# ELU applied to the loaded values of the last layer instead of the evicted ones of the first

## The chip, the cores and the metric

The kernel runs on one core of a Trainium2 chip. Times are device microseconds (us) of that core for one execution. TensorE (PE) does the matrix products, with its weight loads shown apart as PEld; VectorE (DVE), ScalarE (ACT) and GpSimd (POOL) work on elements; SyncE (SP) issues nearly all DMAs. Each engine takes its instructions in the order in which the program holds them.

## What is computed

Attention over 4 x 12 heads with RMS-normed queries and keys gives x (1792 tokens x 768). A capacity-limited mixture of 8 experts maps x to x again. The last stage is two dense layers with an ELU between them, on all tokens:

```python
def _moe2_ref(x, w_in, w_out):          # x 1792 x 768, w_in 768 x 2048, w_out 2048 x 768
    h = x @ w_in
    g = np.where(h > 0.0, h, 1.0 * (np.exp(np.minimum(h, 0.0)) - 1.0))
    return (g @ w_out).astype(np.float32)
```

The change touches this last stage, and a few instructions at the very start of the attention.

## The kernel before

The program runs in three stages: attention up to about 270 us, routing and experts up to about 540 us, the two dense layers to the end. Every float32 operand is split into a high and a low float16 part, and each product is three matmuls: high x high, high x low, low x high.

**Layer 1** (`winograd` called from `fewer`, and `plain`) computes h, transposed: its 2048 rows in pairs f = 0..7 of two 128-row blocks r, its 896 + 896 token columns in two halves h. The first 512 columns of each half go through seven products instead of eight (`winograd`): the accumulators a, b, c take the products in the order A11·B11 into b, A12·B21 into a, S2·T2 onto b, S3·T3 into c, S1·T1 onto b, A22·T4 onto c, S4·B22 onto b. Between them b is copied out twice (`snap`: p1 after the first product, u2 after S2·T2), c once (p7), and each of those copies must be done before the next product goes onto the same accumulator. `add` joins an accumulator with a copy on VectorE, `copy` takes the last one. The other 384 columns go through `plain`, four accumulators of 18 matmuls for each f, spread between the products.

Every finished piece of h (64 pieces: 32 of 512 columns, 32 of 384) goes through `elu`: ACT computes Exp into a tile e, ACT computes Relu(1 - e), DVE takes min(-h, that), which is minus ELU. Then SP stores e to a DRAM buffer `g_d`, laid out by groups of 128 token columns. The tiles e come from five buffers. Two homes for the copies lie in `kept`, inside the tile `sums` (the S operands of layer 1). While layer 1 runs, the weights of both layers are prepared on DVE and ACT.

**Layer 2** takes the tokens in seven groups g of 128 columns of each half. `operands(g)` loads four 128 x 1024 tiles q (one for each k = h + 2r) back from `g_d`, forms four sums s on DVE, and splits seven operands into high (ACT, L1133) and low (DVE, L1134) parts. `layer2` runs the same `winograd` with 24 matmuls of 384 columns for each product; `snap` there is L1245, `add` L1249, `copy` L1252. For g = 0 the piece f = 7 is not loaded but taken from the tiles e that still lie on the chip (`late`), so the sums and splits of g = 0 come in two parts, 7/8 and 1/8.

Three blocks of layer-2 weights come from the DRAM buffer `t_d` just before layer 2: T4 into the old place of x (`xc`), T3 and T1 into the tile `ex`, which takes the place of `sums`, each 1.5 MB. DMAs of SP start in program order, and a DMA whose source is still being stored waits, with all behind it.

The dense layers are placed on the engines by a scheduler: the order within an engine is not the order in the code. `issue_after` holds some instructions back behind another one. The attention's order, in contrast, is written out by hand. At its start a filler (`spin`, L97 to L102) runs 14 matmuls of 512 columns on zeros while the first inputs load.

Of the kernel before, what the change touches and what calls it, by code (L numbers as in the profile page):

```python
# [2 lines left out]

# [3 lines left out]
F32 = mybir.dt.float32  # L7
# [38 lines left out]
def attention(tc, qk_d, v_d, qT_d, idh, idn_d, R_d, xs, L, route, W, npairs=NP_):  # L46
    nc = tc.nc
    order, ramp = ([(s.split(":")[0], int(s.split(":")[1])) for s in x.split()] for x in (ORDER, RAMP))
    with tc.tile_pool(name="ac", bufs=1) as cp, \
# [35 lines left out]
        def first():  # L85

            d = ld[0]
            qk = d["qk"]
            d["r"] = sp.tile([P, 14], F32, tag="r", name="r0", bufs=6)
            sq = d["sq"] = sp.tile([P, 14, D], F32, tag="sq", name="sq0", bufs=1)  # L90
            khl = d["khl"] = sp.tile([P, 7, 2, D], F16, tag="khl", name="khl0")
            for n in ("ss", "ln", "y", "nt"):
                d[n] = sp.tile([P, 14], F32, tag=n, name=n + "0", bufs=4)
            warm, z = pp.tile([P, 512], F32, tag="o", name="warm", bufs=1), ql[1]
            nc.vector.memset(z[:, 0:512], 0.0)

            def spin(n):  # L97
                for _ in range(n):
                    nc.tensor.matmul(warm, z[:, 0:P], z[:, 0:512], start=True, stop=True)

            steps["w"] = spin
            spin(14)  # L102
            for x in (*xh_, *xl_):
                nc.gpsimd.memset(x[:, 448:512], 0.0)
            nc.gpsimd.tensor_tensor(G, idn_[:, P:P + 1], idn_[:, P + 1:P + 2], ALU.mult)
            nc.gpsimd.tensor_scalar(G, G, 0.125 * SQ, None, ALU.mult)
            nc.gpsimd.tensor_tensor(sq[:, Q], qk[:, Q], qk[:, Q], ALU.mult)
            nc.vector.tensor_tensor(sq[:, K], qk[:, K], qk[:, K], ALU.mult)
# [785 lines left out]
def moe(tc, xp, homes, xs, idx, idh, W, rows, ring, w1_d, w2_d, wi_d, wo_d, lin, g_d, t_d, out):  # L894
    nc = tc.nc
    with tc.tile_pool(name="mp", bufs=1, space=PSUM, reuse_waits="tile") as pp:
# [182 lines left out]
        with tc.tile_pool(name="wb", bufs=1, reuse_waits="tile") as wp:  # L1079
# [25 lines left out]
            def operands(g, late=None):  # L1105


                q = [ring.tile([P, 8, P], F32, tag="w2", name=f"q{g}_{k}", bufs=6) for k in (0, 2, 1, 3)]
                s = [W.wstage.tile([P, 8, P], F32, tag="wst", name=f"s{g}_{k}", bufs=5) for k in range(4)]

                n = 7 if late else 8
                for x, k in zip(q, (0, 2, 1, 3)):
                    nc.sync.dma_start(x[:, 0:n], g_d[g, k, :, 0:n])
                    if g == 1:
                        yield
                parts = [(slice(0, n), [x[:, 0:n] for x in q])]
                if late:
                    parts.append((slice(7, 8), [late[k][:, 0:P].unsqueeze(1) for k in (0, 2, 1, 3)]))
                todo, ahead = [], elus[-1].ins if late else None
                held = lambda n: tc.issue_after(ahead) if late and n else ExitStack()  # L1120
                for n, (f, (a11, a12, a21, a22)) in enumerate(parts):
                    s1, s2, s3, s4 = [x[:, f] for x in s]
                    with held(n):
                        nc.vector.tensor_tensor(s1, a21, a22, ALU.add)
                        nc.vector.tensor_tensor(s2, s1, a11, ALU.subtract)
                        nc.vector.tensor_tensor(s3, a11, a21, ALU.subtract)
                        nc.vector.tensor_tensor(s4, a12, s2, ALU.subtract)
                    todo.append((f, dict(zip((A11, A12, S2, S3, S1, A22, S4), (a11, a12, s2, s3, s1, a22, s4)))))
                a = {}

                def split(k, x):
                    for f, z in todo:
                        nc.scalar.activation(x[:, f, 0], z[k], AF.Copy, scale=SG)  # L1133
                        nc.vector.scalar_tensor_tensor(x[:, f, 1], z[k], SG, x[:, f, 0], ALU.mult, ALU.subtract)  # L1134
# [12 lines left out]

            elus = []

            with tc.tile_pool(name="l1", bufs=1, side="right", reuse_waits="tile") as sp:  # L1150
                def elu(f, cb, k, ps, done=False):
# [7 lines left out]
                    return e, nc.sync.dma_start(g_d[g, k, :, f].rearrange("g p c -> p g c"), e.rearrange("p (g c) -> p g c", c=P))  # L1159

                def plain(f):
                    n = CB[1][1] - CB[1][0]
                    for h, r in ((0, 0), (0, 1), (1, 0), (1, 1)):
                        t, bufs = PS[2 - r]
                        ps = pp.tile([P, 512], F32, name=f"l{f}_1{h}{r}", tag=t, bufs=bufs)[:, 0:n]
                        w = wic[f + 8 * r]
                        for d in range(6):
                            for m, (i, j) in enumerate(((0, 0), (0, 1), (1, 0))):
                                nc.tensor.matmul(ps, w[:, i, d * P:(d + 1) * P], xc[1][:, h, d, j], start=d == 0 and m == 0, stop=d == 5 and m == 2)  # L1169
                        yield elu(f, 1, 2 * r + h, ps)[1]  # L1170

                def fewer(f, beside):
                    made = {}
                    x = {A11: xc[0][:, 0, 0:3], A12: xc[0][:, 0, 3:6], A22: xc[0][:, 1, 3:6]} | dict(zip((S1, S3, S2, S4), (sums[0][:, k] for k in range(4))))
                    w = {B11: (f, 0), B21: (f, 384), B22: (f + 8, 384), T1: ((f, 1), 0), T2: ((f, 1), 384), T3: ((f, 3), 0), T4: ((f, 3), 384)}

# [6 lines left out]
                        if p in (A11, S2, S3, A22):  # L1183
                            next(beside)

                    homes = [*kept, sp.tile([P, 512], F32, tag="e", name=f"z{f}", bufs=5)]

                    def snap(ps):
                        z = homes.pop()
                        nc.scalar.activation(z, ps, AF.Copy, scale=CH2)  # L1190
                        return z

                    def add(ps, z, r, h):
                        nc.vector.scalar_tensor_tensor(z, ps, CH2, z, ALU.mult, ALU.add)
                        made[2 * h + r] = elu(f, 0, 2 * h + r, z, True)[0]

                    def copy(ps, r, h):
                        made[2 * h + r] = elu(f, 0, 2 * h + r, ps)[0]

                    winograd(pp, f"l{f}_", 512, product, snap, add, copy)  # L1200
                    return made

                for f in range(8):
                    if f + 1 < 8:
# [18 lines left out]
            with tc.tile_pool(name="l2a", bufs=1, side="right", reuse_waits="tile") as sa, \  # L1223
# [34 lines left out]
                for g in range(7):  # L1258
                    ops = (first, then, operands(g))[min(g, 2)]
                    if g > 1:  # L1260
                        with tc.issue_after(last.ins):
                            next(ops)
                    elif g:
                        next(ops)
                    else:
                        wt[T4] = load_t(T4, flat[0][:, 6144:12288])
                    behind = lambda k: tc.issue_after(elus[-2].ins if g == 0 else snaps[1 if k in (A11, A12) else 2].ins) if g < 2 else ExitStack()
                    a = ops.send((lambda k: place(g, k), behind))
                    layer2(g, a)

# [39 lines left out]
```

## Time and profile before

| | us |
|---|---|
| median of 3 runs | 942.63 |
| lowest, highest | 940.82, 944.12 |
| profiled execution, own time | 941.17 |
| its span, first to last instruction | 939.4 |
| PE busy | 918.9 (98%) |
| DVE busy | 763.2 (81%) |
| ACT busy | 582.6 (62%) |

The profile shows one execution. Busy shares are averages over stages with different limits; a matmul's duration in it includes its way through the array, so that durations of successive matmuls overlap, and the distance between starts is what one costs. Idle time of an engine that nobody waits for costs nothing.

### The profile page before, as it was taken

The numbers are of one execution on the slowest core, as the hardware profiler recorded it, in microseconds if no ns is written. First come the engines' busy times: TensorE is split into PE (matmuls) and PEld (weight loads), VectorE is DVE, ScalarE is ACT, GpSimd is POOL, SyncE is SP. The second block draws the span as 40 slices with busy tenths as digits, with TensorE's granted clock in tenths as the row PEclk, the third lists the DMA queues.
The fourth block names the chain that finished last, engine by engine and source line by source line (L and its number), as shares of the span: only waits on it lengthen the run. The fifth ranks groups of instructions, "written<-read, shape, count | busy, mean of one in ns | idle before, by whom it ended". The sixth has DMA issues, their size and how long they took to land.

```text
span 939.4 us, 18782 instructions
## 1 busy us (share of the span) xinstructions
PE 918.9 (98%) x6855; PEld 614.0 (65%) x6855; DVE 763.2 (81%) x1455; ACT 582.6 (62%) x1251; POOL 370.8 (39%) x552
## 2 busy tenths in 40 slices
PE   7999999999998999999999999999999999999997
PEld 3555555555544899999999955555555566666664
DVE  8999998899868877998888899999999776655430
ACT  7989999999864655566655466666666643333320
POOL 5779999999622200699997000000000001000000
PEclk9999999999998999999999999999999999999999
DMA  9644444453235956887867257777776974232000
GB/s 351 211 111 151 122 141 123 147 165 83 66 83 194 240 185 216 240 228 233 269 218 224 94 187 221 238 226 236 235 230 196 360 265 146 85 105 97 35 35 33
DMA packets 100353, 164.93 MB, mean 176 GB/s; under 512 B 32672, under 2 KB 65952, under 8 KB 99872
## 3 DMA queue, kind: packets, MB, share of 16 engines
q1 hardware_dynamic: 96048, 152.66, 51.9%
q0 software_dynamic: 2400, 11.01, 3.5%
q8 instruction: 55, 0.90, 0.4%
q14 instruction: 42, 0.34, 0.1%
q10 hardware_dynamic: 1808, 0.01, 0.1%
HBM read 131.66 MB, written 31.99 MB: 174 GB/s over the span
## 4 chain that ended last, share of the span: by engine, by line
PE 87%; DVE 6%; POOL 2%; ACT 1%; DMA 1%; issue 1%; POOLq 0%; DVEq 0%; ACTq 0%
PE ph L989 12%; PE py L997 12%; PE o_b L1240 11%; PE l L1169 10%; PE o L320 7%; PE l_b L1181 7%; PE o_c L1240 6%; PE s L243 5%; PE pt L296 4%; PE l_c L1181 3%; PE o_a L1240 3%; PE l_a L1181 2%; DVE s L248 1%; PE xt L948 1%; PE pt L294 1%
## 5 line engine op out<-in xcount | busy, mean ns | idle before, releaser
L1256 POOL DMA_INDIRECT out<-xc,id x14 | 14.6, 1046 | 410.1 <-issue 261.8
L1240 PEld LDWEIGHTS <-a 128*128 128x128 f16 x1080 | 105.7, 98 | 69.8
L1014 DVE SCALAR_TENSOR_TENSOR w<-fw,w 128x768 f16<-128x768 f32 (+1 forms) x90 | 109.3, 1224 | 8.6 <-ACT w L1011 8.4
L997 PE MATMUL py<-h,w 128*128 128x224 f16 x1152 | 114.2, 259 | 0.0
L997 PEld LDWEIGHTS <-w 128*128 128x128 f16 x1152 | 109.8, 98 | 0.2
L248 DVE TENSOR_REDUCE s<-s 128x1 f32<-128x448 f32 x168 | 104.8, 626 | 5.4 <-PE s L243 4.8
L267 ACT ACTIVATE p<-s,nb,r 128x448 f32<-128x448 f32 x144 | 104.4, 726 | 4.1 <-DVE nb L254 3.0
L1169 PE MATMUL l<-xc,wic 128*128 128x384 f16 x576 | 100.3, 326 | 0.0
L989 PE MATMUL ph<-xe,w 128*128 128x224 f16 x1008 | 97.7, 259 | 0.0
L989 PEld LDWEIGHTS <-w 128*128 128x128 f16 x1008 | 96.6, 98 | 0.0
L305 ACT ACTIVATE e<-pt 128x448 f32<-128x448 f32 (+2 forms) x208 | 80.9, 429 | 14.5 <-PE pt L296 14.2
L320 PE MATMUL o<-e,v 128*64 128x448 f32 x384 | 87.8, 558 | 0.0
L1011 ACT ACTIVATE w<-fw 128x768 f16<-128x768 f32 (+1 forms) x90 | 81.7, 921 | 5.7 <-DMA fw<-w 5.7
L1169 PEld LDWEIGHTS <-wic 128*128 128x128 f16 x576 | 56.4, 98 | 41.6
L296 PE MATMUL pt<-idn,p 128*128 128x128 f32 x432 | 70.9, 276 | 0.9 <-ACT p L267 0.9
L296 PEld LDWEIGHTS pt<-idn,p 128*128 128x128 f32 x432 | 50.0, 141 | 23.9 <-ACT e L305 12.3
L1134 DVE SCALAR_TENSOR_TENSOR a<-s,a 128x1024 f16<-128x1024 f32 (+2 forms) x30 | 33.1, 1116 | 33.7 <-ACT a L1133 33.7
L973 POOL TENSOR_TENSOR sums<-sums 128x128 f32<-128x128 f32 (+2 forms) x48 | 58.0, 1208 | 2.8
L243 PE MATMUL s<-ks,qh 128*128 128x448 f16 x144 | 51.2, 355 | 1.9 <-ACT p L267 1.0
L1240 PE MATMUL o_b<-wb,a 128*128 128x384 f16 x312 | 52.0, 326 | 0.0
L243 PE MATMUL s<-ks,ql 128*128 128x448 f16 x144 | 50.7, 352 | 0.0
L961 ACT ACTIVATE xc<-py 128x224 f16<-128x224 f32 (+2 forms) x54 | 18.1, 335 | 51.0 <-PE py L997 46.5
(340 smaller groups left out, 1957.2 us busy)
## 6 DMA issues: line engine op xcount, KB each, us to landing
fw<-w SPq DMA_DIRECT2D x54, 384.0 KB, 3.8
fw<-w SPq DMA_DIRECT2D x36, 512.0 KB, 4.6
xwi<-wi SPq DMA_DIRECT2D x16, 768.0 KB, 7.2
xwo<-wo SPq DMA_DIRECT2D x16, 768.0 KB, 5.1
q<-g_d SPq DMA_DIRECT2D x24, 512.0 KB, 3.7
qT<-qT SPq DMA_DIRECT2D x24, 448.0 KB, 4.2
qk<-qk SPq DMA_DIRECT2D x23, 448.0 KB, 3.5
g_d<-e SPq DMA_DIRECT2D x32, 256.0 KB, 3.7
```

Source lines behind the costliest of these rows:

```text
L243: nc.tensor.matmul(ps[:, 0:448], q[:, o:o + P], ks[:, 448 * h:448 * h + 448], start=n == 0, stop=n == 1)
L248: nc.vector.tensor_reduce(d["s", u][:, 448:449], d["s", u][:, 0:448], AX.X, ALU.max, negate=True)
L267: nc.scalar.activation(dst, d["s", u][:, 0:448], AF.Exp, bias=d["nb", u], scale=d["r"][:, rc:rc + 1], accum_out=d["sm"][:, rc:rc + 1])
L296: nc.tensor.transpose(pt[:, j * P:(j + 1) * P], p[j][:, h, 64 * h + c * P:64 * h + (c + 1) * P], idn)
L320: nc.tensor.matmul(d["o"][64 * h:64 * h + 64, 0:448], d["v"][:, c + 4 * h, :], d["e", min(2 * c + h, 6)], start=c == 0, stop=c == 3)
L989: nc.tensor.matmul(ps, w[:, i, d * P:(d + 1) * P], x[:, d, j], start=d == 0 and n == 0, stop=d == 5 and n == 2)
L997: nc.tensor.matmul(ps, w[:, i, f * P:(f + 1) * P], h[:, f, j], start=f == 0 and n == 0, stop=f == 7 and n == 2)
L1011: nc.scalar.activation(ws[k][:, 0], fs[k], AF.Copy, scale=SW)
L1014: nc.vector.scalar_tensor_tensor(ws[k][:, 1], fs[k], SW, ws[k][:, 0], ALU.mult, ALU.subtract)
L1169: nc.tensor.matmul(ps, w[:, i, d * P:(d + 1) * P], xc[1][:, h, d, j], start=d == 0 and m == 0, stop=d == 5 and m == 2)
L1181: nc.tensor.matmul(ps, wic[k][:, i, c + d * P:c + d * P + P], x[p][:, d, j], start=first and d == 0 and m == 0, stop=d == 2 and m == 2, sk ...
L1240: nc.tensor.matmul(ps, a[x][:, f, i], wt[b][f][:, j], start=first and f == 0 and k == 0, stop=f == 7 and k == 2, skip_group_check=True)
```

## The change

1. `elu` is gone from layer 1. `evict` only copies an accumulator out (ACT Copy, L1170 of the new code), `store` stores it. Of the copies in `winograd`, all three now lie in e tiles from the five buffers, and `add` works in place. What lies in `g_d` is h, not minus ELU of h.
2. `operands` applies the ELU after the load: for each of the four q tiles Exp and Relu on ACT (L1136, L1137, into the place where a sum s will stand later) and the min on DVE (L1138), in place. This stands ahead of the sums and splits. For g = 0 it happens in two parts, for the loaded 7/8 and for the 1/8 from the e tiles.
3. `held` and `behind` name other instructions to wait for (`made`, `copied` in place of `elus`).
4. The 14 filler matmuls at the start become seven pairs: one on rows 0 to 63, one on rows 64 to 127, into two accumulators.

```diff
-            spin(14)
+            beside = pp.tile([P, 512], F32, tag="s", name="warm2", bufs=3)
+            for _ in range(7):
+                for o, x in ((warm, z[0:64]), (beside, z[64:128])):
+                    nc.tensor.matmul(o, x[:, 0:P], x[:, 0:512], start=True, stop=True)
...
-                todo, ahead = [], elus[-1].ins if late else None
...
+                todo, ahead = [], (made[-1].ins, copied[-1].ins) if late else ()
+                for n, (f, raw) in enumerate(parts):
+                    s1, s2, s3, s4 = t = [x[:, f] for x in s]
+                    a11, a12, a21, a22 = y = [x[:, f] for x in q]
                     with held(n):
+                        for o, z, x in zip(y, t, raw):
+                            nc.scalar.activation(z, x, AF.Exp)
+                            nc.scalar.activation(z, z, AF.Relu, bias=1.0, scale=-1.0)
+                            nc.vector.scalar_tensor_tensor(o, x, -1.0, z, ALU.mult, ALU.min)
...
-                    nc.scalar.activation(e, ps, AF.Exp, scale=1.0 if done else CH2)
-                    nc.scalar.activation(e, e, AF.Relu, bias=1.0, scale=-1.0)
-                    elus.append(nc.vector.scalar_tensor_tensor(e, ps, -1.0 if done else -CH2, e, ALU.mult, ALU.min))
+                    return e, nc.scalar.activation(e, ps, AF.Copy, scale=CH2)
...
                     def add(ps, z, r, h):
-                        nc.vector.scalar_tensor_tensor(z, ps, CH2, z, ALU.mult, ALU.add)
-                        made[2 * h + r] = elu(f, 0, 2 * h + r, z, True)[0]
+                        made.append(nc.vector.scalar_tensor_tensor(z, ps, CH2, z, ALU.mult, ALU.add))
+                        store(f, 0, 2 * h + r, z)
+                        late[2 * h + r] = z
```

The scheduler orders the dense layers anew. Three places show what the prediction speaks of. In the names, e7_001 is the piece f = 7 of the first columns (0), h = 0, r = 1 (e7_111 one of the other columns), q1_2 the loaded tile k = 2 of group 1, s1_1 a sum tile of group 1, a1_0 a split operand of group 1, o0_b the accumulator b of layer 2 in group 0, l7_b that of layer 1 in f = 7.

ACT, end of the operands of group 0 and start of those of group 1, before:

```order
L1155 ACTIVATE e7_111_12192<-l7_111_12173 128x384
L1133 ACTIVATE a0_5_12217<-s0_3_12059 128x128
L1156 ACTIVATE e7_111_12192<-e7_111_12192 128x384
L1245 ACTIVATE xc1_6524<-o0_b_12223 128x384 x2
L1133 ACTIVATE a1_0_12406<-q1_0_12114 128x8x128
L1133 ACTIVATE a1_1_12409<-q1_2_12115 128x8x128
L1245 ACTIVATE xc1_6524<-o0_c_12224 128x384
```

The same place after:

```order
L1148 ACTIVATE a0_5_12082<-s0_3_11908 128x128
L1265 ACTIVATE xc1_6525<-o0_b_12088 128x384
L1136 ACTIVATE s1_1_11990<-q1_2_11986 128x1024
L1137 ACTIVATE s1_1_11990<-s1_1_11990 128x1024
L1136 ACTIVATE s1_2_11991<-q1_1_11987 128x1024
L1136 ACTIVATE s1_3_11992<-q1_3_11988 128x1024
L1137 ACTIVATE s1_2_11991<-s1_2_11991 128x1024
L1265 ACTIVATE xc1_6525<-o0_b_12088 128x384
L1148 ACTIVATE a1_0_12283<-q1_0_11985 128x8x128
L1148 ACTIVATE a1_1_12286<-q1_2_11986 128x8x128
L1265 ACTIVATE xc1_6525<-o0_c_12089 128x384
```

The two copies of b in group 0 (p1, then u2) stood next to each other, and now five instructions on loaded tiles of group 1 stand between them.

ACT in f = 7 of layer 1, around its copies u2 and p7, before:

```order
L1156 ACTIVATE e7_000_11982<-e7_000_11982 128x512
L1190 ACTIVATE sums_7684<-l7_b_11960 128x512
L1093 ACTIVATE u34_7_11750<-t34_7_11744 128x2x384
L1190 ACTIVATE sums_7684<-l7_c_11961 128x512
L1133 ACTIVATE xc0_6523<-q0_2_12053 128x7x128
```

The same place after:

```order
L1170 ACTIVATE e6_001_11808<-l6_b_11643 128x512
L1170 ACTIVATE e7_000_11831<-l7_b_11820 128x512
L1136 ACTIVATE s0_1_11906<-q0_2_11902 128x896
L1137 ACTIVATE s0_1_11906<-s0_1_11906 128x896
L1136 ACTIVATE s0_2_11907<-q0_1_11903 128x896
L1136 ACTIVATE s0_3_11908<-q0_3_11904 128x896
L1137 ACTIVATE s0_2_11907<-s0_2_11907 128x896
L1170 ACTIVATE e7_011_11853<-l7_b_11820 128x512
L1170 ACTIVATE e7_010_11864<-l7_c_11821 128x512
```

The copies of b and c (u2 and p7, now e7_011 and e7_010) came ahead of the first split of a loaded tile, and now they come behind five instructions on the loaded tiles of group 0.

SP from the weight loads for layer 2 to the loads of group 1, after:

```order
L1105 DMA xc0_6524<-t_d_67 128x6144
L1175 DMA g_d_66<-e7_010_11864 128x4x128
L1175 DMA g_d_66<-e7_011_11853 128x4x128
L1105 DMA ex_11900<-t_d_67 128x6144 x2
L1175 DMA g_d_66<-e7_001_11897 128x4x128
L1175 DMA g_d_66<-e7_100_11982 128x3x128
L1175 DMA g_d_66<-e7_101_12013 128x3x128
L1175 DMA g_d_66<-e7_110_12036 128x3x128
L1175 DMA g_d_66<-e7_111_12059 128x3x128
L1116 DMA q1_2_11986<-g_d_66 128x1024
L1116 DMA q1_1_11987<-g_d_66 128x1024
L1116 DMA q1_3_11988<-g_d_66 128x1024
```

Before, SP holds the same transfers in this stretch (with e7_011 ahead of e7_010): T4, two stores, T3 and T1, five stores, then the loads of group 1; nothing moved here but what each store waits for.

## Rows read from the trace of the kernel before

**Rows 1.** The page, busy time of the engines, share of the span.

```profile
PE 918.9 (98%) x6855; PEld 614.0 (65%) x6855; DVE 763.2 (81%) x1455; ACT 582.6 (62%) x1251; POOL 370.8 (39%) x552
```

**Rows 2.** Stretches: length, busy PE, PEld, DVE, ACT, POOL (instructions), clock, DMA, GB/s.

```profile
540.00:742.00 202.00, 202.00 (x1082) 105.65 (x1080) 196.59 (x303) 127.59 (x216) 0.00 (x0) 1.00 0.73 229
742.00:934.00 192.00, 191.47 (x1179) 115.06 (x1176) 100.32 (x108) 60.55 (x84) 13.68 (x13) 1.00 0.34 116
```

**Rows 3.** PE's waits in the whole span: total us, times, longest.

```profile
PE warm L1027 <- PEq L726: 1.9, 1, 1.9
```

**Rows 4.** Groups by shape, ACT and DVE, 540 to 935: busy us, mean ns.

```profile
L1155 ACT ACTIVATE e<-l 128x384 f32<-128x384 f32 x32 | 15.4, 484 | 23.6 <-PE l L1169 21.9 <-DMA g_d<-e 1.7
L1155 ACT ACTIVATE e<-l_b 128x512 f32<-128x512 f32 x8 | 4.8, 595 | 4.4 <-PE l_b L1181 4.4
L1133 ACT ACTIVATE a<-q 128x1024 f16<-128x1024 f32 x18 | 19.0, 1054 | 28.4 <-PE o_c L1240 14.0 <-PE o_a L1240 9.7 <-issue 2.5
L1134 DVE SCALAR_TENSOR_TENSOR a<-q,a 128x1024 f16<-128x1024 f32 x18 | 22.0, 1224 | 21.2 <-ACT a L1133 21.2
L1133 ACT ACTIVATE xc<-q 128x896 f16<-128x896 f32 x2 | 1.9, 951 | 3.4 <-DMA q<-g_d 3.4
```

**Rows 5.** Timeline of PE, 714 to 765: start, length, operation, count.

```profile
735.06 2.10 PE L1181 MATMUL l_b<-sums,wic 128*128 128x512 f16 x9
737.00 5.36 PE L1169 MATMUL l<-xc,wic 128*128 128x384 f16 x32
742.20 2.28 PE L1240 MATMUL o_a<-wb,xc 128*128 128x384 f16 x13
...
751.95 4.06 PE L1240 MATMUL o_b<-t,xc 128*128 128x384 f16 x24
...
757.80 4.06 PE L1240 MATMUL o_b<-ex,a 128*128 128x384 f16 x24
```

**Rows 6.** Timeline of ACT, 735 to 765: the copy u2 of group 0, idle before.

```profile
756.05 0.49 ACT L1245 ACTIVATE xc<-o_b 128x384 f32<-128x384 f32 x1 [6.83 <-PE o_b L1240]
```

**Rows 7.** Timeline of SP's issues, 734 to 756: T4, T3 and T1, loads of q.

```profile
735.21 0.32 SPq L1102 DMA_DIRECT2D xc<-t_d  x1
...
738.42 1.73 SPq L1102 DMA_DIRECT2D ex<-t_d  x2
...
753.86 2.30 SPq L1113 DMA_DIRECT2D q<-g_d  x5
```

**Rows 8.** DMA issues, issue to landing: T4; ex; q at 753.86, 725.94; store 722.53; q's spread.

```profile
xc<-t_d SPq DMA_DIRECT2D x1, 1536.0 KB, 8.1
DMA to landing us min/median/max: 10.9/12.5/14.0
q<-g_d SPq DMA_DIRECT2D x1, 512.0 KB, 4.8
q<-g_d SPq DMA_DIRECT2D x1, 448.0 KB, 4.1
g_d<-e SPq DMA_DIRECT2D x1, 256.0 KB, 3.4
DMA to landing us min/median/max: 3.5/3.8/8.1
```

**Rows 9.** Timelines of PE and of its weight loads, start of the program.

```profile
1.33 5.33 PE L99 MATMUL warm<-ql 128*128 128x512 f16 x14 [1.33 <-DVE ql L95]
5.15 0.15 PEld L99 LDWEIGHTS <-ql 128*128 128x128 f16 x1 [0.28 <-issue]
5.58 0.59 PEld L99 LDWEIGHTS <-ql 128*128 128x128 f16 x3 [0.28 <-issue]
7.38 0.40 PE L205 MATMUL pk<-idh,khl 128*128 128x128 f16 x4 [0.72 <-DVE khl L119]
10.77 0.38 PE L236 MATMUL s<-ks,qh 128*64 128x448 f16 x2 [1.12 <-DVE ks L210]
```

**Rows 10.** A stretch near the start, columns as in rows 2.

```profile
7.00:12.00 5.00, 2.89 (x20) 1.41 (x21) 4.96 (x8) 3.24 (x6) 2.48 (x6) 1.00 1.04 409
```

More of the change, by code (lines that the diff above doesn't have):

```diff
@@ L1 @@
-from contextlib import ExitStack
+from contextlib import ExitStack, contextmanager
 from itertools import repeat
@@ L1118, in operands, with held @@
                     parts.append((slice(7, 8), [late[k][:, 0:P].unsqueeze(1) for k in (0, 2, 1, 3)]))
-                todo, ahead = [], elus[-1].ins if late else None
-                held = lambda n: tc.issue_after(ahead) if late and n else ExitStack()
-                for n, (f, (a11, a12, a21, a22)) in enumerate(parts):
-                    s1, s2, s3, s4 = [x[:, f] for x in s]
+                @contextmanager
+                def held(n):
+                    with ExitStack() as x:
+                        for i in ahead if late and n else ():
+                            x.enter_context(tc.issue_after(i))
+                        yield
+                todo, ahead = [], (made[-1].ins, copied[-1].ins) if late else ()
+                for n, (f, raw) in enumerate(parts):
+                    s1, s2, s3, s4 = t = [x[:, f] for x in s]
+                    a11, a12, a21, a22 = y = [x[:, f] for x in q]
                     with held(n):
+                        for o, z, x in zip(y, t, raw):
+                            nc.scalar.activation(z, x, AF.Exp)
+                            nc.scalar.activation(z, z, AF.Relu, bias=1.0, scale=-1.0)
+                            nc.vector.scalar_tensor_tensor(o, x, -1.0, z, ALU.mult, ALU.min)
                         nc.vector.tensor_tensor(s1, a21, a22, ALU.add)
@@ L1146, in operands, with evict @@
                 yield a
-            elus = []
+            made, copied = [], []
             with tc.tile_pool(name="l1", bufs=1, side="right", reuse_waits="tile") as sp:
-                def elu(f, cb, k, ps, done=False):
+                def evict(f, cb, k, ps):
                     c0, c1 = CB[cb]
@@ L1154, in elu, with store @@
                     e = sp.tile([P, 512], F32, tag="e", name=f"e{f}_{cb}{h}{r}", bufs=5)[:, 0:c1 - c0]
-                    nc.scalar.activation(e, ps, AF.Exp, scale=1.0 if done else CH2)
-                    nc.scalar.activation(e, e, AF.Relu, bias=1.0, scale=-1.0)
-                    elus.append(nc.vector.scalar_tensor_tensor(e, ps, -1.0 if done else -CH2, e, ALU.mult, ALU.min))
+                    return e, nc.scalar.activation(e, ps, AF.Copy, scale=CH2)
+                def store(f, cb, k, e):
+                    c0, c1 = CB[cb]
                     g = slice(c0 // P, c1 // P)
-                    return e, nc.sync.dma_start(g_d[g, k, :, f].rearrange("g p c -> p g c"), e.rearrange("p (g c) -> p g c", c=P))
+                    return nc.sync.dma_start(g_d[g, k, :, f].rearrange("g p c -> p g c"), e.rearrange("p (g c) -> p g c", c=P))
                 def plain(f):
@@ L1169, in plain @@
                                 nc.tensor.matmul(ps, w[:, i, d * P:(d + 1) * P], xc[1][:, h, d, j], start=d == 0 and m == 0, stop=d == 5 and m == 2)
-                        yield elu(f, 1, 2 * r + h, ps)[1]
+                        e, x = evict(f, 1, 2 * r + h, ps)
+                        copied.append(x)
+                        yield store(f, 1, 2 * r + h, e)
                 def fewer(f, beside):
-                    made = {}
+                    late = {}
                     x = {A11: xc[0][:, 0, 0:3], A12: xc[0][:, 0, 3:6], A22: xc[0][:, 1, 3:6]} | dict(zip((S1, S3, S2, S4), (sums[0][:, k] for k in range(4))))
@@ L1184, in product @@
                             next(beside)
-                    homes = [*kept, sp.tile([P, 512], F32, tag="e", name=f"z{f}", bufs=5)]
+                    homes = [1, 3, 0]
                     def snap(ps):
-                        z = homes.pop()
-                        nc.scalar.activation(z, ps, AF.Copy, scale=CH2)
-                        return z
+                        return evict(f, 0, homes.pop(), ps)[0]
                     def add(ps, z, r, h):
-                        nc.vector.scalar_tensor_tensor(z, ps, CH2, z, ALU.mult, ALU.add)
-                        made[2 * h + r] = elu(f, 0, 2 * h + r, z, True)[0]
+                        made.append(nc.vector.scalar_tensor_tensor(z, ps, CH2, z, ALU.mult, ALU.add))
+                        store(f, 0, 2 * h + r, z)
+                        late[2 * h + r] = z
                     def copy(ps, r, h):
-                        made[2 * h + r] = elu(f, 0, 2 * h + r, ps)[0]
+                        z, x = evict(f, 0, 2 * h + r, ps)
+                        store(f, 0, 2 * h + r, z)
+                        copied.append(x)
+                        late[2 * h + r] = z
                     winograd(pp, f"l{f}_", 512, product, snap, add, copy)
-                    return made
+                    return late
                 for f in range(8):
@@ L1266, in moe @@
                         wt[T4] = load_t(T4, flat[0][:, 6144:12288])
-                    behind = lambda k: tc.issue_after(elus[-2].ins if g == 0 else snaps[1 if k in (A11, A12) else 2].ins) if g < 2 else ExitStack()
+                    behind = lambda k: tc.issue_after(copied[-2].ins if g == 0 else snaps[1 if k in (A11, A12) else 2].ins) if g < 2 else ExitStack()
                     a = ops.send((lambda k: place(g, k), behind))
```

## The prediction

> **What bounds the kernel now.** I read the page's busy line first: PE works 98% of the span, DVE 81%, ACT 62% [rows 1]. A share is an average, so I looked at the two layers by themselves. In layer 1 (540 to 742) PE is busy 202.00 of 202 us, in layer 2 (742 to 934) 191.47 of 192, at a granted clock of 1.00, the upper of its two levels [rows 2]. PE's waits in the whole span hold none in either layer; the longest, 1.9 us, is in the routing [rows 3]. Pitches say whether small bubbles hide in that. Layer 2 runs 7 x 7 x 24 = 1176 matmuls of 384 columns, one per 191.47/1179 = 0.1624 us. For 512 columns, nine matmuls of S4 reach from 735.06 to 737.00 [rows 5], 0.2155 us each. Layer 1 has 8 x 72 of 384 and 8 x 63 of 512 columns: 8 x (72 x 0.1624 + 63 x 0.2155) = 202.2 us, what the window holds. So both layers are matmuls end to end. Work saved on ACT and DVE can shorten nothing there; what the change can do is make PE wait where it doesn't.
>
> The sum is made against the profiled execution, 941.17 us, which is 1.46 under the median of 942.63. I take the same distance after: predicted median = 942.63 + sum.
>
> **Part 1: ELU gone from layer 1.** ACT loses 64 Exp and 64 Relu and gains 40 copies (32 x 0.484 + 8 x 0.595 = 20.2 us, durations of the same shapes in [rows 4]); DVE loses 64 mins. DVE was busy 196.59 of those 202 us [rows 2], yet PE did not wait for it [rows 3]. Worth to PE: 0.
>
> **Part 2: ELU on the loaded tiles.** Per group ACT gets four Exp and four Relu and DVE four mins of 1024 elements. No row shows these at that size; ACT's 1024-wide split takes 1.054, DVE's 1.224 [rows 4], and I take those: 8 x 1.05 = 8.4 and 4 x 1.22 = 4.9 us. With the rest of a group (ACT 7 splits of 1.05, 4 copies of 0.49; DVE 3 sums of PSUM, 4 sums and 7 splits of about 1.2) ACT has some 17.7 and DVE some 20 us to do, while PE works 168 x 0.1624 = 27.3 us. It fits, and from group 2 on the operands have about a group's time to be made. Cost there: 0, bounded above in the rivals.
>
> **Part 3: the order on ACT, first of layer 2.** ACT takes instructions in order. In group 0 the copy u2 must be out of accumulator b before PE may start S1·T1 on it. Before, it came right after p1, and ACT stood idle 6.83 us ahead of it [rows 6]: free cover. After, three Exp and two Relu on tiles of *group 1* stand between, and the first of them waits until q1_2 has been loaded. So u2 now waits for a DMA, and S1·T1 for u2. Step by step:
> - S4 of f = 7 used to end at 737.00, ahead of 32 matmuls `l` [rows 5]. After, A12, S2 and S4 work in other homes, but PE's order here is kept except that the last 13 matmuls come behind S4's end: 742.2 - 13 x 0.1624 = 740.1, plus the delay of 0.4 of part 4: 740.5.
> - `ex` takes the place of `sums`, which S4 reads last. So T3 and T1 are issued at 740.6 to 741.2, where they were issued from 738.42 [rows 7].
> - They are 1.5 MB each and landed after 10.9 and 14.0 us [rows 8], T3 at 749.3 and T1, issued about 739.0, at 753.0. T4, issued at 735.21 and 8.1 us long [rows 7, 8], shared the DMA engines with them for 4.3 us, and after it shares less. T1 lands at 751.0 to 752.5.
> - The loads of q of group 1 were issued at 753.86 [rows 7], 0.9 after T1's landing, since the store of e7_001 and four more stand between T1 and them, and q must wait for the stores. After: 751.9 to 753.4, middle 752.6.
> - Such a load took 4.8, 4.1 and in the middle of all 3.8 us, the shortest 3.5 [rows 8]. With 4.3, q1_2 is there at 756.9 (755.4 to 758.2).
> - Then ACT: Exp and Relu of q1_2, Exp, Exp, Relu of the next, and u2: 5 x about 1.0 [rows 4] + 0.49 [rows 6] = 5.5 us. u2 ends at 762.4 (760.9 to 763.8).
> - T3 lands about 751 too. PE reaches S3·T3 after 45 matmuls, 742.7 + 0.4 + 7.3 = 750.4, so it may stand there already for up to a microsecond. That is no addition: what PE loses there it no longer loses at S1·T1.
> - PE could start S1·T1 after 96 matmuls of layer 2 (it did, 742.20 to 757.80 [rows 5]): 742.2 + 0.5 + 15.6 = 758.3, the 0.5 being the delay so far.
>
> **Wait: 4.1 us (2.6 to 5.5)**, all on PE's path. Behind u2 on ACT stand the splits of group 1 and the copy p7; p7 is wanted a full product later, and the splits of group 1 more than 10 us later, so I charge nothing more.
>
> **Part 4: the same in f = 7 of layer 1.** There u2 comes behind five instructions on the loaded tiles of *group 0* (0.951 each by the split of that shape [rows 4]), and these tiles want the last store of f = 6 landed. From the end of S4 in f = 6: copy 0.6, store 3.4, load 4.1 [rows 8], five of 0.95, copy 0.6: 13.4 to 13.9 us. PE comes to S1·T1 of f = 7 after four products of 9 and some 35 matmuls `l`, about 13.4 us later by the pitches above. Wait: **0.4 us**, from 0 (the load lands in 3.5) to 1.4 (it takes a microsecond more).
>
> **Part 5: the filler.** Before, 14 matmuls of 512 columns start at 1.33; two weight loads among them stand 0.43 us apart (5.15, 5.58), the pitch of the lower clock level, and the next three fit in 0.59 [rows 9]. So the clock rose inside the filler, at about 5.6. The seven pairs contract half the rows each. If a pair takes two turns, nothing changes: 0. If its halves run side by side, as the two 64-column halves of L236 do in 0.38 us [rows 9], the filler is 7 x 0.43 = 3.0 us long, ends at 4.3, and the clock may rise later. Then the transposes (from 7.38, waiting for DVE by 0.72) and the first scores (10.77, waiting for DVE by 1.12 [rows 9]) run at the lower level. Upper bound: from 7 to 12 us PE is busy 2.89 us [rows 10]; that doubled is 2.9 more, less the 0.72 and 1.12 of waiting: 1.0. Taken: **0.1**, since DVE and not PE is what these matmuls wait for.
>
> The Trainium skill ("TensorE: Matmul & The Clock Gate", "Part 3: Packing small matmuls — row/col tiling") says that matmuls of few contraction rows on different row groups run at the same time. The rows show it for column halves only; by the page the filler is the short one, and the sum would still be the 0.1 taken.
>
> **Sum:** 4.1 + 0.4 + 0.1 = +4.6 us, that is 945.8 for the profiled execution and **947.2** for the median. By the ends of the terms, +2.6 to +7.9: 945.2 to 950.5.
>
> **The rivals.**
>
> *Not slower than can be told: q1_2 comes early.* If the store of e7_001 does not wait in the DMA engines until T3 and T1 are through, the loads of q are held only by SP's order: the store of e7_111 stands ahead of them and wants its copy. Between the copies of e7_001 (done 741.1) and e7_111 ACT has six instructions of 0.95, three copies of 0.48 [rows 4] and ten of 128 columns, which I take at a quarter of 0.95 each: 9.6 us, so 750.7. With a load of 3.5 [rows 8] q1_2 is there at 754.2 to 754.6, u2 ends at 759.7 to 760.1, and PE waits 1.4 to 1.8, with nothing in f = 7 or at the start. Time 944.0 to 945.1, say 944.5. It decides when T1 lands before about 750. For it: 8.1 us for T4, mostly alone, against 14.0 for T1 [rows 8] shows that much of T1's time is sharing. Against it: 753.86 in the profile stands just behind T1 [rows 7]. Chance 0.20.
>
> *Slower by more: the start stays at the lower level.* If the short filler does not lift the clock and the gaps behind it keep it down for another stretch, the 2.9 us of [rows 10] come once or twice, less the 1.8 of waiting: plus 1 to 4 us, 948 to 951. For it: the clock rose late, at 5.6. Against it: with PE busy for only 2.89 of 5 us the granted clock stayed at 1.00 [rows 10]. Chance 0.08.
>
> *Slower by much: every group waits.* If the new ACT work ahead of p1, u2 or p7 delays these copies in each of groups 1 to 6 as in group 0, by some 2 us, 12 us more: 959. Against it: 17.7 of 27.3 us on ACT, and loads issued a group ahead. Chance 0.05.
>
> *Faster.* DVE and ACT free in layer 1 could end waits that the trace hides. No idle PE time stands there to be given back [rows 2, 3]. At most some 0.3 us of 192.00 - 191.47, and the start. Below 939.8 it would need a mechanism that I don't see. Chance 0.04.
>
> **How the numbers follow.** The forecast has 0.63. About 0.3%, 2.8 us, is what a measurement of this kernel can tell from no change: 939.8 to 945.5. Below it I have 0.04. Within it lie the first rival, 0.20, and the low edge of my own range, 0.06: 0.26. Above: 0.57 of the forecast, 0.08 and 0.05: 0.70. The range reaches from 943.2, the first rival's lower end of 944.0 less what a median of three can be off, to 950.4, the upper end of the terms, and leaves out about 0.2: the faster case, the cases of 951 and 959, and some of the edges.
>
> **What would show it.** Right: one wait of PE of about 4 us at S1·T1 of group 0 (758 to 762), released by ACT's copy u2; ACT's first Exp of group 1 waiting for the load of q; T3 and T1 issued near 741; a wait of some 0.4 us at S1·T1 of f = 7; layer 1 still 202 us long; no PE wait in groups 2 to 6; first scores at about 10.8. Wrong: no PE wait at u2 (the loads are not behind T1, or ACT's order is not what sets u2), the transposes or scores later by over 1 us, or PE waits in each group.

## The result, and the profile after

The changed kernel takes 951.29 us (median, 949.53 to 951.38) against 942.63 before: a ratio of 1.0085 with a 95% interval from 1.0065 to 1.0105, or 6 to 10 us slower. The forecast was slower, at 947.2 with a range to 950.4; the time lies above it. The profiled execution took 949.65 us, 8.48 more than the one before, with a span of 947.9.

The page's busy line of the changed kernel shows that PE does the same matmuls in 1.9 us more busy time, and that ACT is a little busier and DVE a little less [rows 1]:

```profile
PE 920.8 (97%) x6855; PEld 614.2 (65%) x6855; DVE 760.9 (80%) x1423; ACT 591.9 (62%) x1227; POOL 376.3 (40%) x552
```

PE's waits, longest first, were the next view. Before, none stood in the two layers [rows 3]. Columns: who waits for whom, total us, times, longest.

```profile
PE o_b L1260 <- ACT xc L1265: 4.6, 1, 4.6
PE pk L208 <- DVE khl L122: 3.2, 1, 3.2
PE warm L1030 <- PEq L729: 1.8, 1, 1.8
...
PE l_b L1199 <- ACT e L1170: 0.6, 1, 0.6
```

The first is the wait at S1·T1 of group 0 for the copy u2, the last the one at S1·T1 of f = 7: the two that were forecast, 4.60 and 0.60 us. The 3.2 at the start follows the shorter filler. Together, 5.2 us of the 8.5 are in the two waits of the layers. PE's timeline shows the rest, in the four rows around the first wait (start, length, operation, count, idle time before); the first is S2·T2, whose result u2 copies:

```profile
754.52 4.06 PE L1260 MATMUL o_b<-t,xc 128*128 128x384 f16 x24
758.42 0.33 PE L1260 MATMUL o_c<-ex,a 128*128 128x384 f16 x1
763.35 7.00 PE L1260 MATMUL o_b<-ex,a 128*128 128x384 f16 x24 [4.60 <-ACT xc L1265]
770.18 0.49 PE L1260 MATMUL o_b<-wb,a 128*128 128x384 f16 x2
```

The 24 matmuls of S1·T1 reach from 763.35 to 770.18, 6.83 us, where they took 3.90 before (757.80 to 761.70 [rows 5] with the pitch of 0.1624). The windows of the changed kernel say why. The columns are those of [rows 2]; the granted clock is the third number from the end.

```profile
742.00:758.00 16.00, 16.00 (x101) 9.66 (x99) 9.97 (x22) 9.74 (x26) 0.00 (x0) 1.00 0.99 329
758.70:763.30 4.60, 0.04 (x1) 0.00 (x0) 1.57 (x2) 4.57 (x7) 0.00 (x0) 0.92 0.76 310
763.40:769.20 5.80, 5.80 (x19) 2.77 (x19) 5.41 (x5) 5.80 (x7) 0.00 (x0) 0.50 0.00 0
769.20:770.20 1.00, 1.00 (x8) 0.52 (x7) 0.00 (x0) 1.00 (x2) 0.00 (x0) 0.93 0.00 0
```

Before the wait the clock is at its upper level. It falls towards the wait's end, and PE then works for 5.8 us at the lower level, 0.50, before the clock rises again. So the wait cost 4.60 us of standing and 2.93 us of matmuls at half speed. The accounting against the trace of before: layer 2 starts 0.78 later (742.98 for 742.20: the 0.60 of f = 7 and 0.18 in small differences), + 4.60 + 2.93 = 8.31; the last product of layer 2 starts 8.48 later (937.88 for 929.40), as much as the span grew, so that 0.17 us are left without an account.

The wait itself went through the steps of the prediction. SP's issues of the changed kernel, columns as in [rows 7]: T3 and T1, the five stores, the loads of q.

```profile
741.10 0.81 SPq L1105 DMA_DIRECT2D ex<-t_d  x2
742.00 9.01 SPq L1175 DMA_DIRECT2D g_d<-e  x5
753.81 1.28 SPq L1116 DMA_DIRECT2D q<-g_d  x3
```

And ACT, in answer to [rows 6]: the five instructions on tiles of group 1 (L1136 is Exp, L1137 is Relu), then u2.

```profile
757.94 1.06 ACT L1136 ACTIVATE s<-q 128x1024 f32<-128x1024 f32 x1 [5.95 <-DMA q<-g_d]
759.03 1.06 ACT L1137 ACTIVATE s<-s 128x1024 f32<-128x1024 f32 x1
759.99 1.99 ACT L1136 ACTIVATE s<-q 128x1024 f32<-128x1024 f32 x2
761.88 1.04 ACT L1137 ACTIVATE s<-s 128x1024 f32<-128x1024 f32 x1
762.83 0.47 ACT L1265 ACTIVATE xc<-o_b 128x384 f32<-128x384 f32 x1
```

ACT stood idle for 5.95 us ahead of the first Exp, while u2 could have run from 758.6 on, when S2·T2 ended (754.52 + 4.06). It ran at 762.83.

What the change was to relieve, it did relieve. In layer 1 (540 to 742) DVE is busy 169.83 us in place of 196.59 and ACT 88.07 in place of 127.59 [rows 2], and PE gained nothing from it:

```profile
540.00:742.00 202.00, 201.40 (x1077) 105.16 (x1075) 169.83 (x247) 88.07 (x137) 0.00 (x0) 1.00 0.74 231
```

### The profile page after: what moved, and what is told of

The parts are those of the page before. It is cut to its first block, busy times and chain, and to the rows that moved or that the text cites. A ratio compares the mean times of both kernels' runs of the same rounds, so it can differ in the third digit from the quotient of the medians.

```text
span 947.9 us, 18684 instructions
## 1 busy us (share of the span) xinstructions
PE 920.8 (97%) x6855; PEld 614.2 (65%) x6855; DVE 760.9 (80%) x1423; ACT 591.9 (62%) x1227; POOL 376.3 (40%) x552
## 4 chain that ended last, share of the span: by engine, by line
PE 64%; DMA 2%; ACT 1%; issue 0%; DVE 0%; POOLq 0%; another core or an unknown queue 0%; ACTq 0%; DVEq 0%; SPq 0%
PE ph L992 12%; PE py L1000 12%; PE o_b L1260 11%; PE l L1185 9%; PE l_b L1199 6%; PE o_c L1260 6%; PE l_c L1199 3%; PE o_a L1260 3%; PE l_a L1199 1%; DMA q<-g_d 1%; PE xt L951 1%; DMA xg<-xs,idx 1%; DMA g_d<-e 0%; DMA out<-xc,id 0%; ACT s L1137 0%
## 5 line engine op out<-in xcount | busy, mean ns | idle before, releaser
L1276 POOL DMA_INDIRECT out<-xc,id x14 | 20.1, 1436 | 413.1 <-ACT a L1148 276.2
L1138 DVE SCALAR_TENSOR_TENSOR q<-q,s 128x1024 f32<-128x1024 f32 (+1 forms) x28 | 33.6, 1202 | 31.9 <-ACT s L1137 31.8
```

## The experiments

The theory: u2 stands behind five instructions that wait for a load; PE waits for u2; the clock falls in that wait and PE pays a second time. Its rivals: the matmuls of S1·T1 are slow because of what the other engines do beside them; the filler at the start costs part of the 8.7 us; something else of the moved ELU costs. Times are given as medians; the kernel before took 942.01, 941.35 and 941.60 us in the three sets of runs, where the forecast and the expectations count from 942.63. Sets differ by up to 1.3 us in that, so a ratio, which is taken inside a set, says more than a difference of medians between sets. Each kernel has one traced execution; what is said of waits and of the clock is read from that one.

### The copies first

```diff
-                        for o, z, x in zip(y, t, raw):
-                            nc.scalar.activation(z, x, AF.Exp)
-                            nc.scalar.activation(z, z, AF.Relu, bias=1.0, scale=-1.0)
+                        for j, (o, z, x) in enumerate(zip(y, t, raw)):
+                            with tc.issue_after(snaps[2].ins) if g == 1 and j else ExitStack():
+                                nc.scalar.activation(z, x, AF.Exp)
+                                nc.scalar.activation(z, z, AF.Relu, bias=1.0, scale=-1.0)
```

> The changed kernel with one thing undone: Exp and Relu of the tiles q1_2, q1_1, q1_3 of group 1 are held on ACT behind the copies u2 and p7 of group 0. Theory (u2 waits on ACT behind these five, and PE's clock falls in the wait): the wait of 4.60 us at S1·T1 of group 0 goes, its 24 matmuls take 3.9 us in place of 6.8, and the time falls from 951.3 by 4.6 + 2.9 to 943.8; the wait of 0.6 in f = 7 stays. Rival A (the slow matmuls of S1·T1 come from what ACT and DVE do beside them, not from the wait): only the wait goes, S1·T1 still takes 6.8 us, 946.7. Rival B (the work is merely put off): a wait of 2 us or more appears in group 1, where the operands now come some 1 us later on ACT while PE is 7 us earlier; 946 or above.

Measured: 943.82 us, ratio 1.0016 (1.0007 to 1.0025), as the theory had it. PE's waits from 540 on, and S1·T1 of group 0 with the product after it:

```profile
PE l_b L1200 <- ACT e L1171: 0.6, 1, 0.6
PE o_b L1261 <- ACT xc L1266: 0.4, 1, 0.4
```

```profile
760.46 4.06 PE L1261 MATMUL o_b<-ex,a 128*128 128x384 f16 x24 [0.42 <-ACT xc L1266]
764.36 0.49 PE L1261 MATMUL o_b<-wb,a 128*128 128x384 f16 x2
```

The wait shrinks from 4.60 to 0.42, and the 24 matmuls take 3.90 us again. Nothing appears in group 1, although its operands are now prepared later: rival B falls. That the low clock went with the wait does not yet part the theory from rival A, since ACT's work at S1·T1 was moved too. The next run does.

### The wait filled with matmuls

```diff
                     def product(ps, x, b, first):
+                        if g == 0 and x == S1:
+                            spare = pp.tile([P, 512], F32, tag="a", name="spare", bufs=2)
+                            with tc.issue_after(s3t3[-1].ins):
+                                for _ in range(28):
+                                    nc.tensor.matmul(spare[:, 0:384], a[A11][:, 0, 0], wt[B11][0][:, 0], start=True, stop=True)
```

> The changed kernel with 28 added matmuls of 384 columns on PE between S3·T3 and S1·T1 of group 0, into an accumulator that nobody reads: 28 x 0.1624 = 4.55 us, just what PE waits there. Theory (the wait costs twice, once as idle time of 4.6 us and once since the clock falls in it): the granted clock stays at 1.00, S1·T1 takes 3.9 us in place of 6.8, and the time falls from 951.3 by 2.9 to 948.4, although PE does more. Rival A (S1·T1 is slow from traffic of the other engines): S1·T1 still takes 6.8, 951.3 or slightly more.

Measured: 948.18 us, ratio 1.0062 (1.0049 to 1.0076). The filler takes the place of the wait, and S1·T1 follows at full speed (timeline of PE):

```profile
760.26 4.71 PE L1262 MATMUL spare<-wb,ex 128*128 128x384 f16 x28
764.82 4.06 PE L1265 MATMUL o_b<-ex,a 128*128 128x384 f16 x24
```

The windows of the two stretches, columns as above:

```profile
760.30:764.80 4.50, 4.50 (x29) 2.71 (x28) 1.94 (x2) 4.50 (x6) 0.00 (x0) 1.00 0.74 301
764.80:768.80 4.00, 4.00 (x27) 2.43 (x25) 3.97 (x5) 4.00 (x6) 0.00 (x0) 1.00 0.02 4
```

ACT and DVE do the same beside S1·T1 as in the changed kernel (busy 4.00 and 3.97 of 4 us), and the clock stays at 1.00. So rival A falls: it was the standing still that cost the speed. PE executes 28 matmuls more, and the kernel is faster than the changed one: its five times (946.38 to 949.44) lie below the other five (949.53 to 951.38), by 3.1 us in the medians and 2.2 by the ratios. The intervals of the ratios overlap, so the time alone would not settle it; the trace does, with the 2.9 us at S1·T1.

### Two and four instructions ahead of u2

The edit is that of the first experiment with `j > 1` (two instructions are left ahead of u2) or `j > 2` (four) in place of `j`.

> The changed kernel with only Exp and Relu of q1_2 left ahead of u2 on ACT; those of q1_1 and q1_3 are held behind u2 and p7. Theory: u2 comes three instructions or 2.85 us earlier, so that PE waits 1.8 us in place of 4.6. What the clock does in a wait of that length is open: if it falls as before, S1·T1 takes 6.8 us and the time is 951.3 - 2.85 = 948.4; if it doesn't fall, 945.5. Rival A (traffic): S1·T1 takes 6.8 us whatever the wait, 948.4.

> The changed kernel with Exp and Relu of q1_2 and of q1_1 left ahead of u2 on ACT, and those of q1_3 held behind u2 and p7: four instructions ahead in place of five, between e3_two_ahead (wait 1.85 us, clock kept) and the changed kernel (wait 4.60 us, clock lost for 2.9 us). Theory: a wait of 3.6 us. What the clock does after a wait of that length is open: kept, 951.3 - 0.95 - 2.9 = 947.4; lost, 950.3.

Measured: 944.20 us (ratio 1.0028, 1.0019 to 1.0037) with two ahead, and 948.29 (1.0075, 1.0061 to 1.0089) with four. S1·T1 in the first, and in the second with the row after it:

```profile
761.26 4.06 PE L1261 MATMUL o_b<-ex,a 128*128 128x384 f16 x24 [1.85 <-ACT xc L1266]
```

```profile
762.29 5.74 PE L1261 MATMUL o_b<-ex,a 128*128 128x384 f16 x24 [3.33 <-ACT xc L1266]
767.87 0.49 PE L1261 MATMUL o_b<-wb,a 128*128 128x384 f16 x2
```

After 1.85 us of standing the matmuls run at full speed. After 3.33 us they take 5.58 us in place of 3.90: 1.68 are lost to the clock, which the windows of that run show at 0.55 from 762.30 to 765.70. It was still at 1.00 when PE began again (762.2 to 762.6) and fell to 0.50 by 762.8, so the low stretch can begin behind the wait that it follows:

```profile
762.30:765.70 3.40, 3.40 (x12) 1.65 (x12) 3.37 (x4) 3.40 (x5) 0.00 (x0) 0.55 0.01 4
```

So the second price is not in proportion to the wait: none at 1.85 us, 1.7 at 3.3. The time with two ahead fits the case without a second price (1.0028 is 2.7 us, expected 945.5 - 942.63 = 2.9). The answer to the question left open for four instructions lies between the two values given.

### The copies first in both layers, with either filler

In `snap` of layer 1 the copies are also collected in a list `taken`, and the condition of the first experiment becomes

```diff
-                            with tc.issue_after(snaps[2].ins) if g == 1 and j else ExitStack():
+                            with tc.issue_after((snaps[2] if g else taken[-1]).ins) if g == 1 and j or late and n == 0 and j else ExitStack():
```

> As e1_copies_first, and in f = 7 of layer 1 Exp and Relu of the loaded tiles q0_2, q0_1, q0_3 are held behind the copies u2 and p7 as well. Theory: the wait of 0.6 us at S1·T1 of f = 7 goes too, 943.2, that is within 0.1% of the kernel before (942.63), with no wait in either layer. Rival (something else of the change still costs): 944.5 or above. Rival (relief of ACT and DVE is worth something after all): below 941.

Measured: 942.28 us, ratio 1.0001 (0.9992 to 1.0010). The waits of PE in the two layers are down to one, of another kind: A11·B11 of group 0 waits for the low 7/8 of its operand (128 x 896), made on DVE.

```profile
PE o_b L1263 <- DVE ex L1150: 0.9, 1, 0.9
```

The theory holds in its time, not in its "no wait in either layer": this wait stands only in the runs in which the operands of group 0 are held too (0.9, 0.9 and 0.5 us), so it is most likely the price of that hold. With the copies ahead, the whole change costs nothing that can be told, and the relief of ACT and DVE is worth nothing that can be told. To see what the filler does, three kernels changed it alone, by putting `spin(14)` in place of the seven pairs or the other way round: in the changed kernel, in the kernel before, and in the kernel just shown, the last beside a second measurement of that one.

> The changed kernel with the start of the kernel before: 14 filler matmuls on all rows in place of seven pairs. Theory (the pairs cost nothing: in the profile of the changed kernel they end 2.2 us earlier, the clock stays low until about 11.3 us, and from 12 us on PE is 0.3 us ahead, which is gone again at 540): the same as the changed kernel, 951.3, with the wait and the low clock of group 0 unchanged. Rival (the low clock at the start costs something that the profiles hide): 949.5 or below.

> The kernel before with the seven pairs at the start and nothing else of the change. Theory: no difference, 942.0 to 942.6. Rival (the pairs cost): 943.5 or above; the opposite rival (the 0.3 us that PE is ahead at 12 us reaches the end): 941.7.

> As e4_both_first (the copies ahead of Exp and Relu of loaded tiles in f = 7 and in group 0), with the 14 filler matmuls of the kernel before at the start: what is left of the change is the ELU moved, and nothing else. Theory (the pairs cost about the 1.1 us, with an interval from 0.3 to 2.0, that they cost alone): 1 us below e4_both_first of the same call, 941.2, and not to be told from the kernel before. Rival (the pairs cost nothing, and the 1.1 us were chance): within 0.4 us of e4_both_first.

> e4_both_first a second time, beside e9_both_first_old on the same chip. Theory: 942.3, 1 us above e9_both_first_old. Rival: within 0.4 us of it.

Measured as ratios to the kernel before: 1.0081 (1.0068 to 1.0095) for the changed kernel with the old filler, where with the pairs it had 1.0085; 1.0012 (1.0003 to 1.0021) for the pairs alone; 1.0002 (0.9992 to 1.0011) and 1.0000 (0.9987 to 1.0013) for the copies first with the old filler and with the pairs, 941.95 and 942.00 us. The 1.1 us of the pairs alone made me expect 1 us between the last two. There is 0.05, so my expectation fell. The closest comparison of the three, the last, shows no cost; that of the changed kernel shows none either, but its two ratios come from different sets and are known only to 0.2%; the pairs alone show 0.1%, clear of zero by their interval. So more than 0.1 to 0.2% is out, and whether the pairs cost 0.1% stays open. Two of the bounds written down mislead here, since they were set as times: the 949.41 us of the changed kernel with the old filler lies below the rival's 949.5, and the 942.45 us of the pairs alone inside the theory's 942.0 to 942.6, but the kernel before took 941.35 in that set, 1.28 less than the bounds assume.

The run of the changed kernel with the old filler also repeats the main finding. Its wait is as long as with the pairs, but the low clock is shorter:

```profile
765.77 5.50 PE L1257 MATMUL o_b<-ex,a 128*128 128x384 f16 x24 [4.57 <-ACT xc L1262]
771.11 0.49 PE L1257 MATMUL o_b<-wb,a 128*128 128x384 f16 x2
```

S1·T1 reaches from 765.77 to 771.11, 5.34 us: 1.4 lost after a wait of 4.57, where the changed kernel lost 2.9 after 4.60. The windows of 1 us show why: here the clock was back at about 768.7 (0.63 from 768 to 769, 1.00 after), 3.0 us after S1·T1 began, and in the changed kernel at about 769.3 (0.83 from 769 to 770), 6.0 us after. So in two executions with the same instructions and nearly the same wait the second price differs by 1.5 us; what decides it is open. The times of the changed kernel lie in two groups, 949.5 to 949.7 and 951.3 to 951.4, 1.7 us apart; that this is the same variation is not shown. The two traces speak against reading it off the times: the execution with the smaller second price took 0.9 us longer (950.58 for 949.65), because its layer 1 began 2.4 us later (539.9 for 537.5).

### An eighth of T1

```diff
-                nc.sync.dma_start(t, t_d[k - T1])
-                return [t[:, f] for f in range(8)]
+                n = 1 if k == T1 else 8
+                nc.sync.dma_start(t[:, 0:n], t_d[k - T1, :, 0:n])
+                return [t[:, f % n] for f in range(8)]
```

Holds on Relu of q1_3 and on Exp and Relu of q2_0 keep the same five instructions ahead of u2.

> The changed kernel, with only an eighth of T1 loaded (0.19 in place of 1.5 MB) and that eighth used for all eight chunks of S1·T1 and of the other groups' products with T1, so that this product isn't the reference's. The same five instructions stand ahead of u2 on ACT; the load of q1_2 stands ahead of the store of e7_111 on SP. Theory (the load of q1_2 waits for the store of e7_001, which shares the DMA engines with T4, T3 and T1 ahead of it): with 1.3 MB less the store lands some 4 us earlier, q1_2 is issued at about 749.5, u2 ends before S1·T1 can start, there is no wait and no low clock, and the time is 943.8. Rival (T1's bytes don't matter; stores and loads of g_d have their own time): q1_2 is issued within a microsecond of 753.8, and the time stays above 949.

Measured: 944.64 us, ratio 1.0041 (1.0024 to 1.0059). The loads of q are issued 3.2 us earlier than in the changed kernel, not 4.3; the first Exp runs at 754.24, and PE still waits 1.95 us, with no slow matmuls after it in the traced execution, which took 943.80 (one of the six, untraced, took 949.13). The rows are from SP's, ACT's (the first two Exp, and u2) and PE's timelines:

```profile
750.58 1.28 SPq L1117 DMA_DIRECT2D q<-g_d  x3
```

```profile
754.24 1.06 ACT L1139 ACTIVATE s<-q 128x1024 f32<-128x1024 f32 x1 [2.53 <-DMA q<-g_d]
755.77 1.06 ACT L1139 ACTIVATE s<-q 128x1024 f32<-128x1024 f32 x1 [0.48 <-DMA q<-g_d]
...
759.88 0.47 ACT L1269 ACTIVATE xc<-o_b 128x384 f32<-128x384 f32 x1
```

```profile
760.40 4.06 PE L1264 MATMUL o_b<-ex,a 128*128 128x384 f16 x24 [1.95 <-ACT xc L1269]
```

So T1's bytes do delay the loads of q, by way of the store of e7_001 behind them: that store, issued at 741.73, landed 8.7 us later, at 750.4, just before the loads were issued, and the other stores behind it landed after them. The theory is right on the cause and not on the size. By the theory u2 would have been out of the way in time. It was not, since q came only at 754.24 and ACT then also waited for the second and the third tile between its instructions (0.48 at 755.77, 0.20 at 757.97).

## Why the prediction was right and wrong

**Bound, parts 1 and 2: right.** PE bounds both layers, and relief of ACT and DVE brought nothing: e9_both_first_old, which is the moved ELU with the order mended, is at 1.0002 of the kernel before. Exp and Relu of 1024 elements take 1.052 and 1.051 us, the min 1.221, as the nearest rows had it [rows 4]. One reading was off, without effect: the 192.00 - 191.47 us are no idle time in layer 2 but the end of the window behind the last matmul (929.40 + 4.06 = 933.46). No wait of PE appears in groups 1 to 6, so the rival of a wait in every group is out.

**Part 3, the wait: right in mechanism, place and size.** Forecast 4.1 (2.6 to 5.5), measured 4.60. Step by step: T3 and T1 issued at 740.6 to 741.2, measured 741.10; loads of q at 751.9 to 753.4, measured 753.81; q1_2 there at 755.4 to 758.2, measured 757.94; the five instructions and u2 5.5 us, measured 5.36; u2 done at 760.9 to 763.8, measured 763.30. One step is off: I let T1's landing move with its issue and shrink since it shares less, and shrank it too far. The loads of q left at 753.81, as before (753.86 [rows 7]), though T3 and T1 were issued 2.7 us later. From 742 to 758 the DMA engines were busy for 0.99 of the time (1.02 before), so it is likely that what lay between T4 and the loads took as long as its bytes took. The run with an eighth of T1 shows that side: 1.3 MB less, 3.2 us earlier. That the wait came out only 0.5 over the forecast owes something to luck: u2 was 0.9 later than its middle, and PE 0.45 later too (758.75 for 758.3).

**Part 3, its last sentence: wrong.** "So I charge nothing more" is the step that failed. The wait cost 7.5 us, 4.60 in it and 2.93 behind it, because PE's clock was at its lower level for the next 5.8 us. The sum with this term would be 4.6 + 0.6 + 2.9 = 8.1, that is 950.7. Three runs hold it up: without the wait the clock stays (e1_copies_first, 943.82 for 943.8 expected), with the wait filled it stays (e2_busy_wait, 948.18 for 948.4), and after a short wait it stays (e3_two_ahead). I had the two levels before me in [rows 9] and asked what the filler does to the clock, but never what a wait in the middle of layer 2 does to it. The Trainium skill speaks of it ("TensorE: Matmul & The Clock Gate", "HAM oscillation — how this bites in real kernels": when PE waits long enough for a load between its matmuls, its clock is lowered, and the next matmuls start slow). The trace agrees, with S1·T1 at half speed for 5.8 us after a wait of 4.60; after 1.85 us in layer 2 the clock stayed up.

The trace of before held a case as well, behind the one wait that I did read [rows 3]:

```profile
302.33 5.44 PE L1027 MATMUL warm<-wa,idh 128*128 128x512 f16 x16 [1.90 <-PEq L726]
```

At the pitch of 0.2155 these 16 matmuls take 3.45 us; they took 5.44, and the granted clock was 0.50 from 300.4 to 306 us. There it had fallen ahead of the wait (0.55 from 299.1 to 300.4), among short matmuls and gaps, so that case is not the same as a single wait behind back-to-back matmuls. But bounds could have been given from it: nothing, or S1·T1 and what follows at twice 0.1624 for some microseconds: 2.0 us by that case (5.44 less 3.45), 3.9 if all of S1·T1 ran so.

**Part 4: right.** 0.60 for 0.4 (0 to 1.4), and it goes when the copies stand ahead.

**Part 5: right on what it costs, as far as 0.1 to 0.2% can be told.** The fourteen half matmuls took 3.17 us in place of 5.33 [rows 9]; seven pairs at 0.43 make 3.0, so the halves of a pair run side by side:

```profile
1.34 3.17 PE L105 MATMUL warm<-ql 64*128 64x512 f16 x14 [1.34 <-DVE ql L95]
```

The Trainium skill says so of matmuls on different row groups ("TensorE: Matmul & The Clock Gate", "Part 3: Packing small matmuls — row/col tiling"). The trace agrees. The clock then was low in the stretch for which I had worked out the upper bound, 0.66 in the mean from 7 to 12 us. The windows from 7 to 30 us, in answer to [rows 10], and PE's timeline at the first scores:

```profile
7.00:12.00 5.00, 4.07 (x20) 1.59 (x21) 4.91 (x8) 3.23 (x7) 2.02 (x7) 0.66 1.03 404
12.00:30.00 18.00, 16.08 (x101) 8.52 (x99) 17.13 (x45) 17.86 (x49) 15.33 (x30) 1.00 1.03 405
```

```profile
10.38 0.58 PE L239 MATMUL s<-ks,qh 128*64 128x448 f16 x2 [0.20 <-DVE ks L213]
```

PE is busy 4.07 us in place of 2.89 for the same work, and this filled idle time: the first scores start at 10.38, earlier than the 10.77 of before, since they wait for DVE. The second rival, a low clock through the first heads, is out: 1.00 from 12 us on. That the time came out at its upper end of 951 is chance: the clock was low in another place and for another reason.

**The first rival** (the loads come early) did not happen, and the run with an eighth of T1 shows that its price was near, a little low: q1_2 at 754.24 (754.2 to 754.6 in the prediction), u2 done at 760.35 (759.7 to 760.1), a wait of 1.95 (1.4 to 1.8). Its times from 944.0 reach up to 945.1, though 942.63 and a wait of 1.8 make only 944.4. By the ratio that run was 3.9 us slower than the kernel before, with the wait of f = 7 still in it (0.5 us), which the rival left out.

## What to carry to other kernels

Where TensorE works without a gap, a wait on it can have two prices: its length, and what the clock takes afterwards. Estimate both, the second with a range that includes nothing, and ask of every instruction that is moved ahead of a copy for PE whether it waits for something that comes later than the copy could run. Saving work on engines that nobody waited for bought nothing here; ordering what is left, so that the copies PE needs come before work that has time, is what decided this change.

## What the runs showed of the hardware

- After PE stood for 1.85 and 1.95 us in layer 2, the 24 matmuls behind it ran at full speed; after 3.33, 4.57 and 4.60 us they lost 1.7, 1.4 and 2.9 us, in one traced execution each. The losses don't follow the lengths: 1.4 us after 4.57, 1.7 after 3.33, and two waits of nearly the same length differ by 1.5 us.
- That 1.9 us cost nothing holds for layer 2 alone, where PE had worked without a gap. In the routing of the changed kernel, where short matmuls and gaps came first, the clock fell just behind a wait of 1.83 us that ended at 301.4 (1.00 to 300.4, 0.85 from there to 302.3, 0.50 to 304), and 16 matmuls of 512 columns took 5.30 us for 3.45.
- Matmuls that nobody reads, put into the wait, kept the clock at 1.00 and made the kernel 2 to 3 us faster (948.18 for 951.29 in the medians, 1.0062 for 1.0085 in the ratios).
- Profiled executions differ ahead of the changed part: the first matmul of layer 1 started at 537.5 us in the profiles of before and after, at 538.8 with the copies first and at 539.9 with the old filler, though their code is the same from behind the filler at the start up to there. A span alone would have misplaced 2 us; the waits and losses above are therefore taken inside a stage.
